# Half of the bf16 quad products and the softmax multiply on GpSimd, and one grouping of the exps throughout

## The chip, the cores and the metric

The kernel runs on one core of a Trainium2 chip. The metric is the device time of one execution in microseconds; the median of several executions is compared. Engines are named as in the profile: PE is TensorE (PEld its weight loads), DVE is VectorE, ACT is ScalarE, POOL is GpSimd, SP is the engine that issues DMAs here.

## The reference

One transformer block with adaptive layer norm: attention with 32 heads of 20 over 2048 tokens of 640, then a bilinear gated unit of width 1536. Everything is bf16.

```python
mod = (_silu(c) @ w_mod).reshape(c.shape[0], 6, 1, -1)
sa, ca, ga, sb, cb, gb = (mod[:, i] for i in range(6))
h = _layernorm(x) * (1 + ca) + sa
qkv = (h @ wqkv).reshape(B, S, 3, 32, 20)           # q, k, v by head
p = _softmax(einsum('bhqd,bhkd->bhqk', q, k) * 20 ** -0.5)
x = x + ga * (einsum('bhqk,bhkd->bhqd', p, v) @ wo)
h = _layernorm(x) * (1 + cb) + sb
x = x + gb * (((h @ w_gate) * (h @ w_up)) @ w_down)
```

(The two middle lines of attention leave out the transposes.) The exponentials are the bulk: 32 heads times 2048 times 2048 scores.

## The kernel before

**Tiling.** The queries are cut into five chunks (`CHUNKS`): three of 512 and two of 256 tokens. The heads are taken four at a time (a set, `j` from 0 to 7), each head in its own 32 rows of the PE array. One chunk and one set make an item; there are 40, taken in order. An item's scores come in units of one PSUM bank: 128 keys by 512 queries, or two times 128 keys by 256 queries. There are 2048 units in all.

**Two ways to an exponential.** Most units go through ACT: exp of a group of two or three neighbouring banks into a buffer `PP` (L1238). The others go through VectorE, four units to a quad (`QUADS` sets how many quads an item has, 93 in all). The queries are scaled beforehand so that a score in PSUM is already in units of a bf16's low bits. For each of the four units, L1262 adds a bias and converts to int16, into one quarter of an input slot of `DB0`. Then three operations over all 2048 elements make two bf16 tensors whose sum, after PV, stands for the exponential: M (L1290) takes the mantissa bits into a slot of `DSS`, X (L1295) multiplies that in place by the same bits read as bf16, and EX (L1298) takes the exponent bits into a second `DSS` slot. `DB0` has two slots (`NB0`), `DSS` three (`NSS`). An input slot is given back when both X and EX have been put in order, and its next user waits for both.

**PSUM.** Exp groups lie alternately in banks 0 to 2 and banks 3 and 4. Bank 7 gathers PV (L1666). Banks 5 and 6 are working banks (`G`), which every projection, transpose and quad unit takes for a while: PE fills one, and VectorE or ACT evicts it. With `HEADG = 60`, the first 60 exp groups have two units each, so that bank 2 isn't needed by them and is a third working bank; it goes back to the exp groups at group 60.

**After PV.** At the end of an item, VectorE transposes bank 7 in 32 by 32 blocks (L1343), takes the reciprocals of the softmax sums (L1346), multiplies (L1348) and transposes back (L1355); DMAs put the result into `Ocp`. When a chunk's items are done, its suffix (output projection, layer norm, gate and up, down projection: L1424 to L1575) is spread over the next chunk's groups; the last chunk's suffix is the tail of the program.

**Projections.** K and V of all tokens and Q of the first chunk are needed early. A K round is either direct (`kq_round`, L878: four heads at 20-row offsets straight into `KT`) or packed (`packed_round`, L929: 128 rows of K at once, stored to DRAM by SP and read back by SP into the layout that the scores need, L978 and L991). `K_DIRECT` names the token tiles (of 512 tokens) whose first set is direct; `K_ALL` those in which all sets are.

**The order.** All of the program is put in order beforehand by a planner in the kernel file (`Sched`). It has a duration for each task, a priority, gates (not before exp group n) and due positions for quad units, and walks through time picking, for each engine, the ready task of the highest priority. The result is one fixed order for each engine with semaphore waits[...]. `steal` (L240) gives ACT an eviction of VectorE's while ACT would be idle, up to `STEAL_END` of the planner's time in ns. Other constants that the change touches: how early K rounds are due (`K_LEAD`, `KD_LEAD`), by which exp group the modulation weights are loaded (`WM_GATE`) and due (`WM_NEED`), how many units a PV batch takes (`PVCAP`), how quads are given precedence (`D_RES`), and how late projections and the suffix are spread (`LATE_L`, `LATEQ_A`, `GATE_F`).

On POOL there are only small things: two memsets of weights, and the layer norms' reciprocal roots on one element per partition (L830, L832, L1445, L1447).

Of the kernel before, what the change touches and what calls it, by code (L numbers as in the profile page):

```python
# [6 lines left out]
ALU = mybir.AluOpType  # L7
AX = mybir.AxisListType
BF16 = mybir.dt.bfloat16
# [12 lines left out]
T0 = 700.0  # L22
DMA_SLOW = 0.0015
DMA_LAT = 1700.0
STEAL_END = 94936.728
STEAL_GAP = 300.0
HAM_W = 3413.3
HAM_MIN = 2550.0
# [85 lines left out]
class Sched:  # L114
# [125 lines left out]
    def steal(self):  # L240
        if self.t > STEAL_END or (self.pend["act"] and self.pend["act"][0][0] < self.t + STEAL_GAP):
            return False
        self.pull("dve")
        best = None
        for task in self.readyl["dve"]:
            if task.alt is not None and (best is None or (task.prio, task.seq) < (best.prio, best.seq)):
                best = task
        if best is None or self.free_at["dve"] <= self.t and best is min(self.readyl["dve"], key=lambda x: (x.prio, x.seq)):
            return False
        if not self.acquire(best, self.t):  # L250
            return False
        self.readyl["dve"].remove(best)
        best.eng = best.ctr = "act"
        best.dur, f = best.alt
        best.emits = [f]
        best.lat = ACT_LAT
        self.finish_issue(best, self.t, best.dur)
        self.free_at["act"] = self.t + best.dur
        self.nsteal += 1
        return True  # L260
# [140 lines left out]
QUADS = [(3, 3, 3, 3, 3, 3, 4, 3), 3, (3, 3, 3, 3, 3, 3, 4, 3), (1, 2, 1, 2, 1, 2, 0, 2), 1]  # L401
D_LEAD = 0.35
NB0, NSS = 2, 3
HEADG = 60
GU_ONE = 0
XCONT = 0
T3_POOL = 0
HEAD_OUT = 1
NPS = 4
TS_4X, TT_2X = 600.0, 1145.0  # L410
WM_GATE = 18
WM_NEED = 1.721
K_DIRECT = (0, 1, 2, 3)
Q_DIRECT = 2
K_LEAD = 0.567
K_ALL = (0, 1)
KD_LEAD = 0.559
DMA_WINDOW = 900000
D_LATE = 12
D_RES = 92  # L420
PVMIN, PVMAX, PVCAP = 2, 11, 18
GATE_F = [0.8, 0.893, 0.938, 0.5, 1.0]
FILL_MIN = 4200.0
DUP_MIN = 0.0
XN_POOL = ()
# [4 lines left out]
HT_L = 0.072  # L430
V_L = 0
LATE_A = 1.174
LATE_L = 2.164
LATEQ = (3,)
LATEQ_A = 7
LATEQ_F = 0.73
QUAD_GAIN = 0.597233983857778
NTERM = 2
# [10 lines left out]
def build_kernel(nc, A_x, A_wqkv, A_wo, B_x, B_w_gate, B_w_up, B_w_down, c, w_mod, out):  # L449
# [14 lines left out]
    sc = Sched()  # L464
# [4 lines left out]
    def at(name, shape, dtype, off):  # L469
        cnt[0] += 1  # L470
        return nc.alloc_sbuf_tensor_at(f"{name}_{cnt[0]}", list(shape), dtype, offset=off, align_bytes=32)
# [79 lines left out]
    DB0 = at("DB0", [128, NB0, 4 * 512], I16, d_off)  # L551
    DSS = at("DSS", [128, NSS, 4 * 512], I16, d_off + NB0 * 4096)
# [65 lines left out]

    G = Slots([5, 6, 2] if HEADG else [5, 6], "G")
    GX = Slots([3, 4] if HEADG else [2, 3, 4], "GX")  # L620
    hx = (1, 3) if HEADG else (1, 3, 4)
    GC = Slots([0, 1], "GC")
# [8 lines left out]
    sB0 = Slots(list(range(NB0)), "B0")  # L631
# [15 lines left out]
    def pool(dur, f, deps=(), prio=3.0, **k):  # L647
        return sc.add(Task("pool", dur, f, deps, prio=prio, **k))
# [27 lines left out]
    def load_wm(v, buf, eng, prio, deps=(), gate=0):  # L676
        d_wm[v] = (dma(eng, 128 * KD * D * 2, lambda e: e.dma_start(buf[:, :, :], wmv[:, :, v * D:(v + 1) * D]),
                       deps, prio=prio, dur=550.0, gate=gate), buf)
# [244 lines left out]
    def k_base(tc):  # L923
        return 80 if tc in K_DIRECT else 0

    def nblk(tc):
        return -(-(D - k_base(tc)) // 128)
# [148 lines left out]
    while ap < NA:  # L1076
        even = len(glist) % 2 == 0
        us = ubuf[ap:ap + (3 if even and len(glist) >= HEADG else 2)]
        apos.append(ap)
# [9 lines left out]
    def need(x):  # L1089
        return 13 + 10 * x  # L1090
    q_zero = {}
    for tc in range(4):
        ln1(tc, 2.0 + tc)
        if tc == 0:
            load_rest()
            load_wm(3, wm_a[0], "sp", 9, [r_sa.last] + chained[-2:-1], WM_GATE)
            load_wm(4, wm_a[1], "sp", 9.1, [r_ca.last] + chained[-1:], WM_GATE + 2)
        hT_rounds(tc, 10 if tc == 0 else need(tc / 4 - HT_L))
# [5 lines left out]
        if tc == 3:  # L1104
            x0_done = [t for l in t_xn.values() for t in l]
    r_sb = col_round(3, 2, need(WM_NEED), False)
    r_cb = col_round(4, 3, need(WM_NEED + .05), True)
    load_wm(2, wm_b[0], "sp", 8, x0_done, WM_GATE + 8)
    load_wm(5, wm_b[1], "sp", 9, x0_done, WM_GATE + 12)

# [19 lines left out]
    sc_use = []  # L1130
    ev_ga = gab_round(2, 0, need(WM_NEED + .5))
    ev_gb = gab_round(5, 1, need(WM_NEED + .55))

    z_oc = [pool(1200, lambda e, i=i: e.memset(Ocp[:, i, KD - 1, :], 0.0), [x for l in tr_last.values() for x in l], prio=9)
            for i in range(2)]
    for tc in range(0 if Q_DIRECT < NSET else 1, 4):
        q_zero[tc] = [dma("sp", 12 * H * 1024, lambda e, tc=tc: e.dma_start(
            bass.AP(QS.tensor, (1024 * tc + DH) * 512, [[32 * 512, H], [512, 12], [1, 512]]),
            Ocp[48:80, 1, KD - 1, :].unsqueeze(1).to_broadcast([H, 12, 512])), [z_oc[1], d_wm[4][0]], prio=9.5,
            dur=720.0, gate=WM_GATE + 20 + 12 * tc)]  # L1140

    for tc in range(4):
        if tc > 0 and tc in K_DIRECT:
            kq_round("K", 0, tc, need(tc / 4))
# [6 lines left out]
    for b in range(4 if Q_DIRECT < NSET else 0):  # L1151
        j0 = -(-(160 + b * 128 - 79) // 80)
        late.append((j0 - .05 - K_LEAD, 2560, lambda p, g, b=b: packed_round("Q", b, 0, p, g)))
    for tc in range(4):
        for j in range(1, NSET if tc in K_ALL else 0):
            late.append((j + tc / 4 - KD_LEAD, 2560, lambda p, g, j=j, tc=tc: kq_round("K", j, tc, p, g)))
        for b in range(0 if tc in K_ALL else nblk(tc)):
            r0 = b * 128 + k_base(tc)
            j0 = max(0 if tc not in K_DIRECT else 1, -(-(r0 - 91) // 80))
            late.append((j0 + tc / 4 - K_LEAD, 2560, lambda p, g, b=b, tc=tc: packed_round("K", b, tc, p, g)))  # L1160
    for t in range(NT):
# [7 lines left out]
    for i, (nd, w, f) in enumerate(late):  # L1169
        even = LATE_A + (NSET - LATE_A) * acc / tot  # L1170
        f(need(nd), int(gi * max(0.0, min(nd - LATE_L, even))))
        acc += w
    ql = [(tc, b) for tc in LATEQ for b in range(KD)]
    for i, (tc, b) in enumerate(ql):
        packed_round("Q", b, tc, 500 + i, int(gstart[1] + LATEQ_A + gpc[1] * LATEQ_F * i / len(ql)), True)

# [3 lines left out]
            prio=10),  # L1180
# [39 lines left out]
    for g, (us, b0) in enumerate(glist):  # L1220
        bset = setA if b0 == 0 else setB
        ems = []
        deps = []
# [32 lines left out]
    for qi, (it, us) in enumerate(dquads):  # L1256
        st_ = d_state[qi]
# [11 lines left out]
    for qi, (it, us) in enumerate(dquads):  # L1269
        st_ = d_state[qi]  # L1270
        st_["src"], st_["ss"] = {}, {}

        def term(f, deps, dur, name, slot=None, src=None, last=False, it=it, qi=qi, st_=st_):
            t = Task("dve", dur, f, deps, prio=2.5 + .001 * qi, name=f"{name}.{qi}")
            if slot is not None:
                t.acq = [(sSS, "s", 1)]
            t.cond = lambda: it <= st_pv["item"]

            def on_t(task):
                if slot is not None:  # L1280
                    st_["ss"][slot] = task.slots["s"]
                if last:
                    sB0.done(st_["slot"], task)
                if src is not None:
                    st_["src"][src] = [task]
            t.on_start = on_t
            return sc.add(t)

        def fm(e, st_=st_):
            return e.tensor_scalar(DSS[:, st_["ss"][0], :], DB0[:, st_["slot"], :], 0x7F, 0x3F00, op0=ALU.bitwise_and,  # L1290
                                   op1=ALU.bitwise_or)

        def fx(e, st_=st_):
            d = DSS[:, st_["ss"][0], :].bitcast(BF16)
            return e.tensor_tensor(d, DB0[:, st_["slot"], :].bitcast(BF16), d, ALU.mult)  # L1295

        def fe(e, st_=st_):
            return e.tensor_scalar(DSS[:, st_["ss"][1], :], DB0[:, st_["slot"], :], 0x7F80, 2, op0=ALU.bitwise_and,  # L1298
                                   op1=ALU.bitwise_or)
        tm = term(fm, list(st_["p1"]), TS_4X, "M", slot=0)  # L1300
        term(fx, [tm], TT_2X, "X", src=0, last=True)
        term(fe, list(st_["p1"]), TS_4X, "EX", slot=1, src=1, last=True)

    first_pv = {}
# [32 lines left out]
    def item_end_tasks(it):  # L1337
# [12 lines left out]
            invT[:, 0:nb32].unsqueeze(2).to_broadcast([128, nb32, 32]), ALU.mult)  # L1350
        if T3_POOL and it < len(items) - 1:
            t3 = pool(n * 2.2 + 200, f3, [t2], prio=0)
# [35 lines left out]
    def suffix(ci):  # L1388
# [17 lines left out]
        def gate(w):  # L1406
            g = gb + 9 + int((gl - 9) * GATE_F[ci] * rc_[1] / w_tot)
            rc_[0] += 1
            rc_[1] += w
            return 0 if tail else g  # L1410
# [324 lines left out]
    def d_wants():  # L1735
        g = pvstate["sidx"]
        return g < NG and dst["next"] < len(dlist) and due[dst["next"]] + D_RES < apos[g]

# [75 lines left out]
    def pick_pe(t):  # L1814
        sc.pull("pe")
        g = pvstate["sidx"]
        if HEADG and g >= HEADG - HEAD_OUT and 2 not in G.gone:
            G.retire(2)
        if g < NG:
            ts, us = score_q[g]  # L1820
            if HEADG and g == HEADG and 2 in G.out:
                ts.deps = ts.deps + G.out.pop(2)
# [154 lines left out]
```

The softmax here doesn't subtract the row's maximum and nothing guards it: scores larger than these inputs give would overflow.

## Time and profile before

| | |
|---|---|
| time, median of 3 (lowest to highest) | 843.85 us (842.52 to 844.39) |
| the profiled execution: time, span | 844.39 us, 842.6 us |
| granted PE clock, mean | 0.986 |
| first exp, end of last exp (timeline) | 17.4 us, 807.8 us |
| exps on ACT; quads; quad units | 683; 93; 372 |
| DMA moved, mean | 52.77 MB, 63 GB/s |

"Busy" is time in which an engine has an instruction under way, and "span" runs from the first instruction to the last. The granted clock is the share of full speed that PE was given. In a row of groups, the figures behind the bar are the group's busy time in us, the mean ns of one instruction, and the idle time of the engine just before them with what ended it.

### The profile page before, as it was taken

To read this page: it belongs to the slowest core of one execution; us is meant where nothing else is said; L and a number is where in the kernel's file an instruction comes from. 1 tells how busy PE (TensorE), PEld (TensorE's weight loads), DVE (VectorE), ACT (ScalarE), POOL (GpSimd) and SP (SyncE) were. 2 spreads that over 40 slices of the span, in tenths; PEclk is the share of its full clock that TensorE was granted. 3 is DMA by queue.
4 is the path that set the end of the run, shared out by engine and by line. 5 is a ranking of instruction groups with operands and counts; after the bars stand their busy time and mean duration, and the time that the engine had idled before them with its cause. 6 is when DMAs were issued, how large, how long until landed. Compare 5 with 4: busy or idle time off the path is not lost.

```text
span 842.6 us, 28098 instructions
## 1 busy us (share of the span) xinstructions
PE 794.3 (94%) x12268; PEld 306.1 (36%) x12268; DVE 714.1 (85%) x1266; ACT 783.0 (93%) x719; POOL 31.6 (4%) x65
## 2 busy tenths in 40 slices
PE   8999989999999999999999999999999999998998
PEld 4433333222233222223333222233244433454477
DVE  7997989888999988898789988989779969677773
ACT  4788999998999999999999999999999999999931
POOL 2300000000002000000002000000000000000000
PEclk9998999998999999999999999999999999999999
DMA  9244210012250122310400211000300237124420
GB/s 300 61 139 118 69 43 17 28 47 84 65 123 15 45 57 64 93 57 22 99 2 5 53 45 44 20 12 13 99 4 5 62 77 135 38 65 95 108 59 19
DMA packets 113890, 52.77 MB, mean 63 GB/s; under 512 B 83232, under 2 KB 113768, under 8 KB 113768
## 3 DMA queue, kind: packets, MB, share of 16 engines
q1 hardware_dynamic: 112839, 49.83, 23.3%
q8 instruction: 97, 1.59, 0.8%
q10 hardware_dynamic: 928, 1.15, 0.4%
q14 instruction: 26, 0.20, 0.1%
HBM read 40.83 MB, written 7.82 MB: 58 GB/s over the span
## 4 chain that ended last, share of the span: by engine, by line
PE 49%; ACT 22%; DVE 20%; issue 8%; POOL 0%; ACTq 0%; DVEq 0%
ACT PP L1238 22%; PE ps_all L768 17%; PE ps_all L1204 15%; PE ps_all L1666 11%; DVE DB L1262 7%; PE ps_all L935 3%; DVE DSS L1295 2%; PE ps_all L883 2%; DVE DSS L1290 1%; DVE st L823 1%; DVE DSS L1298 1%; DVE xck L1432 1%; DVE OT L1343 1%; DVE st L1442 1%; PE ps_all L850 1%
## 5 line engine op out<-in xcount | busy, mean ns | idle before, releaser
L1238 ACT ACTIVATE PP<-ps_all 128x1024 bf16<-128x1024 f32 (+2 forms) x683 | 763.9, 1297 | 11.2 <-PE ps_all L1204 10.3
L1204 PE MATMUL ps_all<-QT,KT 32*128 32x512 bf16 (+1 forms) x2560 | 308.6, 341 | 26.4 <-ACT PP L1238 21.6
L1262 DVE TENSOR_SCALAR DB<-ps_all 128x512 int16<-128x512 f32 x372 | 250.6, 682 | 65.5 <-PE ps_all L1204 63.6
L1204 PEld LDWEIGHTS ps_all<-QT,KT 32*128 32x128 bf16 x2560 | 82.6, 91 | 263.0 <-ACT PP L1238 189.5
L1666 PE MATMUL ps_all<-PP,Vf 128*32 128x512 bf16 (+2 forms) x2112 | 166.4, 345 | 0.6 <-issue 0.4
L768 PE MATMUL ps_all<-h2T,stg 128*32 128x512 bf16 x1440 | 111.2, 382 | 4.8 <-DVE DB L1262 3.4
L1295 DVE TENSOR_TENSOR DSS<-DB,DSS 128x2048 bf16<-128x2048 bf16 x93 | 112.6, 1211 | 0.1
L1666 PEld LDWEIGHTS ps_all<-PP,Vf 128*32 128x32 bf16 (+1 forms) x2112 | 48.0, 94 | 88.5 <-issue 80.2
L1666 PE MATMUL ps_all<-DSS,Vf 128*32 128x512 bf16 (+3 forms) x896 | 75.2, 353 | 0.0
L1290 DVE TENSOR_SCALAR DSS<-DB 128x2048 int16<-128x2048 int16 x93 | 63.3, 681 | 1.4
L1298 DVE TENSOR_SCALAR DSS<-DB 128x2048 int16<-128x2048 int16 x93 | 63.3, 681 | 0.8 <-PE ps_all L1666 0.8
L768 PE MATMUL ps_all<-wd,hprod 128*32 128x320 bf16 x1152 | 57.1, 301 | 1.3 <-DVE DB L1262 0.7
L768 PEld LDWEIGHTS ps_all<-h2T,stg 128*32 128x32 bf16 x1440 | 33.7, 95 | 41.8 <-issue 14.5
L1343 DVE STREAM_TRANSPOSE OT<-ps_all 128x512 f32<-128x512 f32 (+1 forms) x40 | 24.2, 605 | 13.4 <-PE ps_all L1666 13.3
L768 PEld LDWEIGHTS ps_all<-wd,hprod 128*32 128x32 bf16 x1152 | 27.7, 96 | 20.5 <-issue 8.8
L768 PE MATMUL ps_all<-wo,Ocp 128*32 128x320 bf16 x640 | 33.4, 302 | 0.6 <-DVE xck L1432 0.2
L1535 DVE CAST gsb<-ps_all 128x512 bf16<-128x512 f32 (+1 forms) x48 | 29.4, 612 | 4.2 <-PE ps_all L768 4.0
L1445 POOL TENSOR_SCALAR sd<-mv 128x1 f32<-128x1 f32 x14 | 5.8, 416 | 698.9 <-DVE mv L1444 698.9
L768 PE MATMUL ps_all<-wV,hT 128*32 128x320 bf16 x640 | 31.1, 306 | 0.3 <-DVE DB L1262 0.2
L935 PE MATMUL ps_all<-hT,wq 128*32 128x512 bf16 x375 | 30.1, 400 | 1.0 <-DVE DB L1262 1.0
L1666 PEld LDWEIGHTS ps_all<-DSS,Vf 128*32 128x32 bf16 (+1 forms) x896 | 23.1, 96 | 20.8 <-issue 11.0
L1546 DVE TENSOR_TENSOR hprod<-ps_all,gsb 128x512 bf16<-128x512 f32 x36 | 24.6, 682 | 4.4 <-PE ps_all L768 4.1
(108 smaller groups left out, 527.0 us busy)
## 6 DMA issues: line engine op xcount, KB each, us to landing
stg<-in_B_w_gate_dram SPq DMA_DIRECT2D x50, 160.0 KB
stg<-in_B_w_up_dram SPq DMA_DIRECT2D x50, 160.0 KB
QT<-q_rows SPq DMA_DIRECT2D x22, 128.0 KB
wm<-in_w_mod_dram SPq DMA_DIRECT2D x3, 800.0 KB
x<-in_A_x_dram SPq DMA_DIRECT2D x7, 320.0 KB
xck<-in_A_x_dram SPq DMA_DIRECT2D x3, 640.0 KB
wd<-in_B_w_down_dram SPq DMA_DIRECT2D x1, 1920.0 KB
out_dram<-xck SPq DMA_DIRECT2D x12, 160.0 KB
```

The source lines that it names most:

```text
L768: return lambda e, b: e.matmul(ps[32 * x:32 * x + 32, b, c0:c0 + n], lhs()[:, 32 * x:32 * x + 32], rhs(), tile_position=(0, 32 * x), start ...
L935: f = [lambda e, b_, k=k, x=x: e.matmul(ps[x:x + min(32, w - x), b_, :], wx[:, k, r0 + x:r0 + min(x + 32, w)], hT[tc][:, k, :], tile_posit ...
L1204: ems.append(lambda e, i=i, kt=kt: e.matmul(dstf()[:, i * u.n:(i + 1) * u.n], KT[32 * u.s:32 * u.s + 32, u.j, kt * 128:(kt + 1) * 128], QT ...
L1238: return e.activation(PPs[g % 2][:, cellp["p"], 0:nu * 512], ps[:, b0:b0 + nu, :].rearrange("p b c -> p (b c)"), AFT.Exp, scale=ESCALE)
L1262: return e.tensor_scalar(DB0[:, st_["slot"], x * 512:(x + 1) * 512], bank(cell["b"]), EBIAS, 0.0, op0=ALU.add, op1=ALU.max)
L1290: return e.tensor_scalar(DSS[:, st_["ss"][0], :], DB0[:, st_["slot"], :], 0x7F, 0x3F00, op0=ALU.bitwise_and, op1=ALU.bitwise_or)
L1295: return e.tensor_tensor(d, DB0[:, st_["slot"], :].bitcast(BF16), d, ALU.mult)
L1298: return e.tensor_scalar(DSS[:, st_["ss"][1], :], DB0[:, st_["slot"], :], 0x7F80, 2, op0=ALU.bitwise_and, op1=ALU.bitwise_or)
L1343: t1 = Task("dve", n * 1.1 + 70, lambda e: e.transpose(OT[:, 0:n], ps[:, BPV, 0:n]), [], prio=0.0, name=f"T1.{it}")
L1535: f = lambda e: e.tensor_copy(gsb[:, gs, 0:n], ps[:, r.b["b"], 0:n])
L1546: f = lambda e: e.tensor_tensor(hprod[:, fc, 0:n], ps[:, r.b["b"], 0:n], gsb[:, gs, 0:n], ALU.mult)
L1666: ems.append(lambda e, i=i, kt=kt, stt=stt, stp=stp: e.matmul(ps[32 * s:32 * s + mc, BPV, 0:u.n], Vf[:, (kt * H + 4 * u.j + s) * VW:(kt * ...
```

## The change

Four edits. The grouping: `HEADG = 0`, so that exp groups are of three and two banks by turns from the first, banks 5 and 6 are the only working banks while exps run, and bank 2 serves only for some first transposes. The product: for every quad of even number, X is done by POOL in four pieces of 512 elements, each a task of its own with the piece before as its dependency; the input slot is given back with the last piece, and PV of the product waits for it. M and EX of these quads, and all of the others, stay on VectorE. The multiply: with `T3_POOL = 1`, L1348 is done by POOL for every item but the last. The constants: `K_DIRECT` keeps token tiles 0 and 1, so that the first set of tiles 2 and 3 is made by packed rounds as well (their first packed round then starts at row 0 and not at row 80); and others that move due times and gates.

```diff
-STEAL_END = 94936.728
+STEAL_END = 60000.0
...
-HEADG = 60
+HEADG = 0
+X_POOL, X_PIECES, POOL_NS = 2, 4, 2.2
 GU_ONE = 0
 XCONT = 0
-T3_POOL = 0
-HEAD_OUT = 1
+T3_POOL = 1
+HEAD_OUT = 2
...
-WM_GATE = 18
-WM_NEED = 1.721
-K_DIRECT = (0, 1, 2, 3)
+WM_GATE = 16
+WM_NEED = 1.802
+K_DIRECT = (0, 1)
...
-K_LEAD = 0.567
+K_LEAD = 0.577
...
-KD_LEAD = 0.559
+KD_LEAD = 0.431
...
-D_RES = 92
-PVMIN, PVMAX, PVCAP = 2, 11, 18
-GATE_F = [0.8, 0.893, 0.938, 0.5, 1.0]
+D_RES = 100
+PVMIN, PVMAX, PVCAP = 2, 11, 16
+GATE_F = [0.8, 0.95, 0.819, 0.5, 1.0]
...
-LATE_L = 2.164
+LATE_L = 2.08
...
-LATEQ_A = 7
+LATEQ_A = 6
...
         tm = term(fm, list(st_["p1"]), TS_4X, "M", slot=0)
-        term(fx, [tm], TT_2X, "X", src=0, last=True)
+        if X_POOL and qi % X_POOL == 0:
+            deps = [tm]
+            for x in range(X_PIECES):
+                w = 2048 // X_PIECES
+
+                def fxp(e, x=x, w=w, st_=st_):
+                    d = DSS[:, st_["ss"][0], x * w:x * w + w].bitcast(BF16)
+                    return e.tensor_tensor(d, DB0[:, st_["slot"], x * w:x * w + w].bitcast(BF16), d, ALU.mult)
+                t = Task("pool", w * POOL_NS + 150.0, fxp, deps, prio=.1 * qi, name=f"XP.{qi}")
+
+                def on_p(task, x=x, st_=st_):
+                    if x == X_PIECES - 1:
+                        sB0.done(st_["slot"], task)
+                        st_["src"][0] = [task]
+                t.on_start = on_p
+                sc.add(t)
+                deps = [t]
+        else:
+            term(fx, [tm], TT_2X, "X", src=0, last=True)
         term(fe, list(st_["p1"]), TS_4X, "EX", slot=1, src=1, last=True)
```

## The prediction, before the changed kernel was run

> **What bounds the kernel now.** I read the busy times first, then the windows by stage, then the groups, then the waits. The columns of the windows are: stretch, its length, then busy us (instructions) of PE, PEld, DVE, ACT, POOL, then granted clock, DMA share, GB/s.
>
> ```profile
> PE 794.3 (94%) x12268; PEld 306.1 (36%) x12268; DVE 714.1 (85%) x1266; ACT 783.0 (93%) x719; POOL 31.6 (4%) x65
> ...
> 20.00:40.00 20.00, 19.55 (x342) 10.09 (x342) 18.67 (x52) 15.27 (x20) 8.39 (x19) 1.00 0.27 79
> 40.00:60.00 20.00, 19.42 (x269) 7.93 (x267) 18.03 (x29) 16.31 (x21) 0.99 (x2) 0.91 0.42 132
> 60.00:80.00 20.00, 20.00 (x246) 6.26 (x244) 15.51 (x27) 17.08 (x19) 0.00 (x0) 0.83 0.42 110
> 300.00:400.00 100.00, 95.14 (x1267) 30.31 (x1259) 89.42 (x144) 99.98 (x90) 0.00 (x0) 1.00 0.22 60
> 500.00:600.00 100.00, 95.20 (x1240) 30.54 (x1232) 88.30 (x136) 99.98 (x90) 0.00 (x0) 1.00 0.12 30
> 780.00:842.60 62.60, 57.06 (x1624) 39.92 (x1612) 37.70 (x85) 32.30 (x38) 1.22 (x2) 1.00 0.27 63
> ```
>
> Two stages are to be seen. From about 100 to 780 us ACT is full (99.98 of 100): a gain on another engine buys nothing there, and only a delay that reaches ACT counts. Before 100 us PE is full with projections and ACT is idle 3 to 5 us in each 20; exp time lost there is never made good. After the last exp (about 808 us) comes a tail of PE and VectorE work.
>
> ```profile
> L1238 ACT ACTIVATE PP<-ps_all 128x1536 bf16<-128x1536 f32 x311 | 477.0, 1534 | 4.5 <-PE ps_all L1204 3.7 <-PE ps_all L1666 0.2
> L1238 ACT ACTIVATE PP<-ps_all 128x1024 bf16<-128x1024 f32 x371 | 403.0, 1101 | 6.8 <-PE ps_all L1204 6.7
> L1262 DVE TENSOR_SCALAR DB<-ps_all 128x512 int16<-128x512 f32 x372 | 250.6, 682 | 65.5 <-PE ps_all L1204 63.6
> L1295 DVE TENSOR_TENSOR DSS<-DB,DSS 128x2048 bf16<-128x2048 bf16 x93 | 112.6, 1211 | 0.1
> L1290 DVE TENSOR_SCALAR DSS<-DB 128x2048 int16<-128x2048 int16 x93 | 63.3, 681 | 1.4
> L1298 DVE TENSOR_SCALAR DSS<-DB 128x2048 int16<-128x2048 int16 x93 | 63.3, 681 | 0.8 <-PE ps_all L1666 0.8
> L1348 DVE TENSOR_TENSOR OTn<-OT,invT 128x512 bf16<-128x512 f32 x24 | 16.4, 683 | 0.1
> ...
> L883 PE MATMUL ps_all<-hT,wk 128*32 128x512 bf16 x360 | 24.9, 381 | 1.8 <-DVE DB L1262 1.1 <-DVE hT L858 0.6
> ```
>
> ```profile
> DVE DB L1262 <- PE ps_all L1204: 63.6, 80, 2.5
> PE ps_all L1204 <- ACT PP L1238: 21.6, 57, 0.9
> ACT PP L1238 <- PE ps_all L1204: 10.3, 11, 3.0
> PE ps_all L768 <- DVE DB L1262: 6.7, 19, 0.7
> ```
>
> The groups give each operation's price; the waits say that VectorE rarely holds up PE (6.7 us on the largest matmul line), that it waits 63.6 us for scores itself, and that PE waits for ACT more than ACT for PE. The product (L1295) has no consumer in the list of large waits.
>
> [...]
>
> **The change, part by part.** Profiled execution: 844.4 us against a span of 842.6, so 1.8 lie outside; the median is 843.85, 0.5 lower. I work on the profiled one and carry the difference over.
>
> *Exp groups.* 2048 score banks less 372 on VectorE leave 1676. With 60 groups of two and then 2.5 on average: 60 + 1556/2.5 = 683, as counted; without, 671. The pitch near the end is 30.18 us for 27 exps of mean 2.5 banks, 1.118; at 60 us it is 13.36/14 = 0.954 for two banks. The line through these has 0.33 a bank and 0.3 fixed, but the second pitch still holds PE waits; two-bank and three-bank durations (1101, 1534) give 0.433 a bank, so a fixed 1.118 − 1.083 = 0.035 to 0.1. Twelve fewer: −0.4 to −1.2, all where ACT isn't the bound. I take −0.5.
>
> *Two working banks in place of three in the head.* From 33 to 53 us, the line windows count 10 first steps of quads, 4 K or packed rounds, 6 V rounds and 8 transpose rounds. Fill plus eviction by the timeline: 0.39 + 0.68 = 1.07; 1.25 + 0.68 = 1.93; 0.72 + 0.48 = 1.2; 0.4 + 0.6 = 1.0. Together 10.7 + 7.7 + 7.2 + 8.0 = 33.6 bank-us in 20 us, 1.7 banks with no queue; with an estimated 0.5 us for semaphores and half an instruction's queue on each of 28, 47.6, or 2.4 banks. So two banks cost between nothing (16.8 us fits into 20) and 3.8 us here, and perhaps half of that in the neighbouring stretches: 0 to +6, I take +3. DVE at 18 of 20 us makes a queue likely.
>
> *K rounds.* K of token tiles 2 and 3 for the first heads is no longer computed directly: 18 direct rounds (360 matmuls) become 16, while the 10 packed rounds stay. Two rounds of 1.25 us go where PE is full: −2.5. Instead these K tiles go through two DMAs and DRAM; in the timeline the SP queue takes 0.34 for a store and 1.91 for four loads to issue alone. ACT has only 7.9 us of exps between 33 and 53 us, so scores are short just where they come later: 0 to +4, I take +2. The ACT steal limit (95 to 60 us) moves one K eviction of 0.58 us in that range to VectorE: nothing.
>
> *Product on GpSimd, 47 of 93 quads.* VectorE loses 47 × 1.13 (the pitch in the chain) = 53 us, and 24 × 0.6 + 15 × 0.33 = 19 us of L1348, 72 together. [...]
>
> Who waits behind a held instruction: the next L1262 on VectorE, with it a working bank, then PE's next filling of that bank, and the next scores behind it in PE's order. [...] PE is idle 5 us per 100 and the exp buffers cover some. [...] I take one in fifteen, +4 to +5: +4, since 89 of 100 us on VectorE leave room for most.
>
> *Later product.* [...] Quads come every 7.7 us (52 first steps per 100 us) and there are two slots, so it just fits. The order places consumers after a planned 4 × 1.276 = 5.1 us. [...] I take +1. What a lighter VectorE gives back to PE in the calm half of the time: −1. [...]
>
> Sum: −0.5 + 3 − 2.5 + 2 + 4 + 1 − 1 = +6. 844.4 + 6 = 850.4 profiled, about 850 as a median.
>
> **Rivals.**
> 1. [...] Late pieces hold the input slot, the next quad's L1262 blocks at the head of VectorE's order, and PE and ACT follow. [...] Against: only every second quad. At 0.4 us per pool quad through to ACT, 19 us: 862.
> 2. *Faster.* VectorE's relief is real [...]: of the 72 us, enough reaches PE before 100 us, where ACT idles about 12 us, to save 4; the K rounds bring 2.5 and the banks cost 2: 844.4 − 4.5, about 839.5. [...] For it: VectorE 18 to 18.7 of 20 us in the head. Against: few quads lie in the head, and the middle has at most some 4 us of ACT idle to win.
> 3. *Nothing shows.* ACT hides the middle, and banks and K rounds cancel: 844.
>
> **How the numbers follow.** Forecast (845.5 to 856) 0.50, rival 1 (above 856) 0.19, rival 2 (under 842.2) 0.22, rival 3 within 0.2% (842.2 to 845.5, about what a measurement of this kernel can tell from no change) 0.09. Slower is 0.50 + 0.19 = 0.69. The range leaves about 0.08 on either side: 840 to 863. The forecast's own is 845.5 to 856.
>
> **What would show it.** 671 exps; [...] ACT under 99.98 of 100 in the middle; the 33 to 53 us stretch with fewer exps. Wrong would be: ACT still full from 100 us on with the exps ending no later than 808 us; or an exp end put off mostly by a wait for POOL on PE, not by VectorE's queue.

## The result, and the profile after

The changed kernel takes 881.69 us (median of 4, 881.43 to 883.30) against 844.12 (842.52 to 845.03): ratio 1.0451, 95% interval 1.0431 to 1.0472. That is 37.6 us slower, where 6 were forecast. The profiled execution has a span of 879.9 us. One execution each of b_t3, a_h60nopool and a_exfirst below was in a slower state: the ratios leave it out, the medians don't (without it they are 855.05, 846.81 and 885.47 us).

The page of the changed kernel, busy time and chain by engine (chain before: PE 49%, ACT 22%, DVE 20%):

```profile
PE 817.3 (93%) x12272; PEld 313.0 (36%) x12272; DVE 682.7 (78%) x1185; ACT 784.6 (89%) x700; POOL 308.0 (35%) x292
...
PE 49%; DVE 26%; ACT 15%; issue 6%; POOL 1%; DMA 1%; POOLq 0%; ACTq 0%; DVEq 0%
```

VectorE is busy 31 us less, and yet it holds a larger share of the chain; ACT, which was the bound, holds less. Windows of the changed kernel, columns as before:

```profile
20.00:40.00 20.00, 17.21 (x312) 9.00 (x309) 17.32 (x50) 13.12 (x15) 8.27 (x19) 1.00 0.16 43
40.00:60.00 20.00, 17.98 (x233) 6.88 (x225) 13.58 (x22) 11.98 (x11) 4.33 (x5) 0.83 0.35 110
60.00:80.00 20.00, 16.80 (x172) 4.50 (x164) 16.02 (x24) 14.31 (x13) 10.05 (x7) 0.84 0.54 157
...
300.00:400.00 100.00, 96.64 (x1194) 29.43 (x1186) 83.64 (x133) 99.19 (x88) 36.54 (x29) 1.00 0.25 65
...
500.00:600.00 100.00, 94.91 (x1187) 28.71 (x1187) 79.25 (x121) 97.52 (x86) 34.30 (x28) 0.98 0.14 33
```

In the head PE is no longer full (16.8 to 18 of 20 us against 19.4 to 20), and ACT gets less. In the middle VectorE is down to 79 to 84 of 100 us, and ACT is no longer quite full. The groups that answer to those shown before, shapes kept apart:

```profile
L1239 ACT ACTIVATE PP<-ps_all 128x1536 bf16<-128x1536 f32 x335 | 496.8, 1483 | 32.1 <-PE ps_all L1205 21.7 <-PE ps_all L1685 8.8
L1239 ACT ACTIVATE PP<-ps_all 128x1024 bf16<-128x1024 f32 x335 | 355.1, 1060 | 7.1 <-PE ps_all L1205 5.4 <-PE ps_all L1685 1.2
L1263 DVE TENSOR_SCALAR DB<-ps_all 128x512 int16<-128x512 f32 x372 | 251.1, 683 | 96.3 <-PE ps_all L1205 95.5
L1309 POOL TENSOR_TENSOR DSS<-DB,DSS 128x512 bf16<-128x512 bf16 x188 | 235.8, 1254 | 271.7 <-DVE DSS L1291 261.4
L1299 DVE TENSOR_SCALAR DSS<-DB 128x2048 int16<-128x2048 int16 x93 | 79.1, 851 | 0.6 <-PE ps_all L1685 0.6
L1291 DVE TENSOR_SCALAR DSS<-DB 128x2048 int16<-128x2048 int16 x93 | 70.0, 753 | 1.7
L1296 DVE TENSOR_TENSOR DSS<-DB,DSS 128x2048 bf16<-128x2048 bf16 x46 | 56.8, 1235 | 0.0
L1367 POOL TENSOR_TENSOR OTn<-OT,invT 128x512 bf16<-128x512 f32 x24 | 33.8, 1407 | 129.7 <-DVE invT L1365 129.7
```

EX (L1299) has grown from 681 to 851 ns, M (L1291) from 681 to 753. What they lose isn't idle time in front of an instruction (0.6 and 1.7 us in all); it is inside its duration. The view of the one line gives least, median and longest in ns:

```profile
L1299 DVE TENSOR_SCALAR DSS<-DB x93: 630/686/1647, 56.3 to 837.9; 128x2048 int16<-128x2048 int16 x93
```

Before, it was 646/683/694: the median is all but the same, and a few are held. 27 EX, 11 M and 3 X take over 0.06 us more than the longest before, 0.57 us more in the mean; the longest EX takes 0.95 us more, where a GpSimd piece takes 1.155. One of them in the timeline (start and length in us first), with a softmax multiply on GpSimd:

```profile
350.98 1.37 POOL L1367 TENSOR_TENSOR OTn<-OT,invT 128x512 bf16<-128x512 f32 x1 [3.22 <-DVE invT L1365]
...
351.36 1.53 DVE L1299 TENSOR_SCALAR DSS<-DB 128x2048 int16<-128x2048 int16 x1
352.82 0.68 DVE L1263 TENSOR_SCALAR DB<-ps_all 128x512 int16<-128x512 f32 x1
```

The multiply ends at 352.35 us and EX 0.55 later. So it is with all 41: each meets a GpSimd multiply that has more than 0.2 us to go and ends at a set distance behind that multiply's end, 0.55 us for EX and M and 1.08 for X. The 14 EX and M that began with less than 0.2 us of one left took 0.67 to 0.74 us. L1263, which reads PSUM, isn't held: 110 of its 372 began with more than 0.2 us of such a multiply left and took 684 ns in the mean, 693 at most, against 682 for those with no GpSimd work beside them. The texts on record call such a hold a lock.

Counted against undisturbed rows, M, EX and X lose 93 × 0.072 + 93 × 0.170 + 46 × 0.025 = 23.7 us. Other VectorE rows grew as well (the layer norm's xn and xn2t of L1468 by 3.8 us, the scaling of `wo` by 0.7), so that all holds are nearer 28. The waits:

```profile
DVE DB L1263 <- PE ps_all L1205: 95.5, 133, 2.4
...
ACT PP L1239 <- PE ps_all L1205: 27.1, 38, 2.8
...
PE ps_all L1205 <- ACT PP L1239: 11.8, 39, 0.6
...
PE ps_all L769 <- DVE DB L1263: 7.4, 18, 1.0
...
DVE OcT L1374 <- POOL OTn L1367: 4.2, 10, 0.7
```

The relation of ACT and PE is turned round: ACT waits 27.1 us for scores (10.3 before), PE 11.8 for ACT (21.6 before). VectorE waits 95.5 us for scores (63.6 before): it has more time and nothing to do with it. No engine has a wait in the list that the product (L1309) ended.

Where it is lost: exps alone, by stage (columns: stretch, length, ACT busy and instructions, granted clock, DMA share, GB/s). The kernel before, then the changed one:

```profile
0.00:100.00 100.00, 61.03 (x64) 0.93 0.49 140
100.00:240.00 140.00, 136.72 (x122) 0.98 0.19 52
240.00:800.00 560.00, 558.34 (x492) 1.00 0.22 53
```

```profile
0.00:100.00 100.00, 54.61 (x47) 0.91 0.44 130
100.00:240.00 140.00, 126.53 (x111) 0.93 0.19 51
240.00:800.00 560.00, 546.99 (x479) 0.99 0.21 51
```

Exp time missing: 6.4, 10.2 and 11.4 us, 28 in all. The last exp ends at 841.1 us against 807.8, 33.3 later: the other 5 us are that the exps as a whole take 769.1 us and not 763.9. The tail behind the last exp lasts 38.8 us against 34.8, 4.0 more.

### The profile page after: what moved, and what is told of

Its sections match the earlier page's. It is cut to its first block, busy times and chain, and to the rows that moved or that the text cites. A ratio compares the mean times of both kernels' runs of the same rounds, so it can differ in the third digit from the quotient of the medians.

```text
span 879.9 us, 28227 instructions
## 1 busy us (share of the span) xinstructions
PE 817.3 (93%) x12272; PEld 313.0 (36%) x12272; DVE 682.7 (78%) x1185; ACT 784.6 (89%) x700; POOL 308.0 (35%) x292
## 4 chain that ended last, share of the span: by engine, by line
PE 49%; DVE 26%; ACT 15%; issue 6%; POOL 1%; DMA 1%; POOLq 0%; ACTq 0%; DVEq 0%
PE ps_all L1205 16%; PE ps_all L769 16%; ACT PP L1239 15%; PE ps_all L1685 11%; DVE DB L1263 9%; PE ps_all L936 3%; DVE DSS L1291 3%; DVE DSS L1299 2%; PE ps_all L884 2%; DVE OT L1362 1%; DVE DSS L1296 1%; DVE st L824 1%; DVE st L1461 1%; PE ps_all L1923 1%; DMA wm<-in_w_mod_dram 1%
## 5 line engine op out<-in xcount | busy, mean ns | idle before, releaser
L1239 ACT ACTIVATE PP<-ps_all 128x1536 bf16<-128x1536 f32 (+1 forms) x671 | 769.1, 1271 | 39.2 <-PE ps_all L1205 27.1
L1205 PE MATMUL ps_all<-QT,KT 32*128 32x512 bf16 (+1 forms) x2560 | 317.4, 345 | 23.9 <-ACT PP L1239 11.8
L1309 POOL TENSOR_TENSOR DSS<-DB,DSS 128x512 bf16<-128x512 bf16 x188 | 235.8, 1254 | 271.7 <-DVE DSS L1291 261.4
L1263 DVE TENSOR_SCALAR DB<-ps_all 128x512 int16<-128x512 f32 x372 | 251.1, 683 | 96.3 <-PE ps_all L1205 95.5
L1367 POOL TENSOR_TENSOR OTn<-OT,invT 128x512 bf16<-128x512 f32 (+1 forms) x39 | 44.9, 1151 | 205.8 <-DVE invT L1365 205.8
L1299 DVE TENSOR_SCALAR DSS<-DB 128x2048 int16<-128x2048 int16 x93 | 79.1, 851 | 0.6 <-PE ps_all L1685 0.6
L1291 DVE TENSOR_SCALAR DSS<-DB 128x2048 int16<-128x2048 int16 x93 | 70.0, 753 | 1.7
L1296 DVE TENSOR_TENSOR DSS<-DB,DSS 128x2048 bf16<-128x2048 bf16 x46 | 56.8, 1235 | 0.0
L769 PE MATMUL ps_all<-wd,hprod 128*32 128x320 bf16 x1152 | 54.6, 301 | 0.5 <-DVE DB L1263 0.3
L1554 DVE CAST gsb<-ps_all 128x512 bf16<-128x512 f32 (+1 forms) x48 | 29.5, 614 | 11.5 <-PE ps_all L769 11.4
L1923 PE MATMUL ps_all<-ident 128*128 128x512 bf16 x84 | 30.5, 422 | 5.6 <-DVE DB L1263 1.9
L936 PE MATMUL ps_all<-hT,wq 128*32 128x512 bf16 x375 | 32.6, 422 | 2.1 <-DVE DB L1263 0.9
```

The source lines that it names most:

```text
L769: return lambda e, b: e.matmul(ps[32 * x:32 * x + 32, b, c0:c0 + n], lhs()[:, 32 * x:32 * x + 32], rhs(), tile_position=(0, 32 * x), start ...
L936: f = [lambda e, b_, k=k, x=x: e.matmul(ps[x:x + min(32, w - x), b_, :], wx[:, k, r0 + x:r0 + min(x + 32, w)], hT[tc][:, k, :], tile_posit ...
L1205: ems.append(lambda e, i=i, kt=kt: e.matmul(dstf()[:, i * u.n:(i + 1) * u.n], KT[32 * u.s:32 * u.s + 32, u.j, kt * 128:(kt + 1) * 128], QT ...
L1239: return e.activation(PPs[g % 2][:, cellp["p"], 0:nu * 512], ps[:, b0:b0 + nu, :].rearrange("p b c -> p (b c)"), AFT.Exp, scale=ESCALE)
L1263: return e.tensor_scalar(DB0[:, st_["slot"], x * 512:(x + 1) * 512], bank(cell["b"]), EBIAS, 0.0, op0=ALU.add, op1=ALU.max)
L1309: return e.tensor_tensor(d, DB0[:, st_["slot"], x * w:x * w + w].bitcast(BF16), d, ALU.mult)
```

## The experiments

All times are medians, with the kernel before run beside them on the same chip. From chip to chip the median of the kernel before lay between 841.30 and 844.12 us, so that a difference of two runs from different chips is good to some 3 us only. "Held" is what M, EX and X took in the profiled execution beyond 681, 681 and 1210 ns each.

| run | what | us | ratio to before (95%) | held, us |
|---|---|---|---|---|
| after | the change | 881.69 | 1.0451 (1.0431–1.0472) | 23.7 |
| a_nopool | change without GpSimd parts | 853.79 | 1.0127 (1.0099–1.0156) | 0 |
| a_head60 | change with 60 groups of two | 869.87 | 1.0342 (1.0283–1.0401) | 28.2 |
| a_h60nopool | other constants alone | 846.95 | 1.0035 (1.0010–1.0060) | 0 |
| b_head0 | grouping alone, old constants | 861.89 | 1.0233 (1.0199–1.0267) | 0 |
| b_xt3 | both GpSimd parts alone | 871.59 | 1.0352 (1.0320–1.0383) | 23.6 |
| b_x | products alone | 865.50 | 1.0272 (1.0245–1.0299) | 20.4 |
| b_t3 | softmax multiply alone | 856.80 | 1.0148 (1.0103–1.0193) | 9.6 |
| b_dummy | before, idle GpSimd multiplies | 872.53 | 1.0351 (1.0318–1.0383) | 31.7 |
| b_memset | before, idle GpSimd memsets | 847.19 | 1.0059 (1.0040–1.0077) | 4.4 |
| b_pad | before, small VectorE pads | 856.46 | 1.0174 (1.0139–1.0208) | – |
| b_lump | before, few large VectorE pads | 867.93 | 1.0304 (1.0263–1.0345) | – |
| a_cut | after, pieces cut to 8 elements | 869.32 | 1.0331 (1.0302–1.0360) | 3.7 |
| a_cut2 | and the multiply cut | 858.43 | 1.0205 (1.0160–1.0251) | 0 |
| a_memset | after, pieces as memsets | 866.84 | 1.0302 (1.0258–1.0347) | 5.7 |
| a_one | after, one piece | 986.06 | 1.1722 (1.1667–1.1777) | 97.4 |
| a_eight | after, eight pieces | 887.31 | 1.0533 (1.0489–1.0576) | 17.1 |
| a_exfirst | after, EX ahead of M | 885.55 | 1.0479 (1.0407–1.0552) | 19.3 |

**Which part of the change.** Four runs undo a part of the change or do one alone. In their expectations "pool" puts the 37 us down to the GpSimd parts, "banks" to the two working banks.

```diff
a_nopool:  -X_POOL, X_PIECES, POOL_NS = 2, 4, 2.2
           +X_POOL, X_PIECES, POOL_NS = 0, 4, 2.2
           -T3_POOL = 1
           +T3_POOL = 0
```

> The changed kernel with both GpSimd parts undone (products and multiply back on VectorE); grouping and constants stay as changed. Theory 'pool' [...]: 848 to 855 us. Theory 'banks' (they come from two working banks before 240 us): 868 to 880 us. If the two share it about evenly: some 862.

```diff
a_head60:  -HEADG = 0
           +HEADG = 60
           -HEAD_OUT = 2
           +HEAD_OUT = 1
```

> The changed kernel with the first 60 exp groups in two banks each again (three working banks in the head); GpSimd work and constants stay as changed. Theory 'pool': 873 to 880 us. Theory 'banks': 850 to 860 us, with the exps done by 240 us near those of the kernel before (194 against 165).

b_xt3 puts the changed kernel's lines for X into the kernel before, and sets `T3_POOL = 1`.

> The kernel before with the two GpSimd parts alone: products of even quads and the softmax multiply on GpSimd, old grouping and old constants. Theory 'pool': 865 to 880 us, with ACT under 98 of 100 us in the middle. Theory 'banks': 846 to 853 us. [...]

b_head0 sets `HEADG = 0` in the kernel before.

> The kernel before with the grouping alone: groups of three and two from the first, two working banks; no GpSimd work, old constants. Theory 'banks': 862 to 880 us, lost before 240 us. Theory 'pool': 845 to 850 us. The old constants were written down for three banks, so that this kernel may also be slower than the changed one without GpSimd.

In b_xt3 M and EX take 735 and 862 ns. The GpSimd parts cost 881.69 − 853.79 = 27.9 us on top of the new grouping, and 871.59 − 842.60 = 29.0 on top of the old: about the same, whatever the grouping. The grouping and the constants are worth 853.79 − 842.60 = 11.2 us. "Pool" is the larger part and "banks" the smaller; a_head60 (869.87) lies between its two expectations, as both count. A later run took the constants by themselves (`HEADG = 60`, `HEAD_OUT = 1`, `X_POOL` and `T3_POOL` at 0 in the changed kernel):

> The changed kernel with neither the grouping nor the GpSimd parts: what is left of the change are the other constants alone. If they cost nothing: 840 to 846 us, and the grouping is the 11 us between this and 853.8. If they carry a part: 847 to 853 us.

846.95 lies between the two expectations: 4.6 over the 842.32 beside it, 3 by the ratio. So some 7 us are the grouping's with these constants; with the old ones it costs 19.3. The exps of a_nopool by stage show where:

```profile
0.00:100.00 100.00, 52.72 (x46) 0.90 0.44 132
100.00:240.00 140.00, 138.97 (x123) 0.99 0.21 58
240.00:800.00 560.00, 554.52 (x489) 0.98 0.21 52
```

The grouping loses its time before 100 us (52.72 against 61.03, and 62.96 with the constants alone), and nothing between 100 and 240. There PE has 72.9 of the 80 us from 20 to 100 with two working banks, 78.8 with three. The GpSimd parts take theirs after 100 us: 138.97 − 126.53 = 12.4 and 554.52 − 546.99 = 7.5.

**The two GpSimd parts apart.** b_t3 sets `T3_POOL = 1` in the kernel before, b_x brings only the products.

> The kernel before with the softmax multiply alone on GpSimd (39 of 40), products on VectorE. Both theories of the products expect little: 841 to 848 us. [...]

> The kernel before with the products of even quads alone on GpSimd; the softmax multiply stays on VectorE. If the products carry the loss of the GpSimd parts: 865 to 873 us, as both together (871.6).

Both count: 12.5 us (8.7 to 16.3) and 22.9 by the ratios, more than the 29 together. The multiply was a miss. Its 39 operations are on GpSimd for 42 us in all (1.35 and 0.67 us each), yet M and EX are held for 9.6 us, and the transpose back waits 3.6 us for its result (nothing before).

**Hold or late product.** b_dummy keeps the kernel before and its orders and adds GpSimd work for which nobody waits.

```diff
     end = sc.run()
+    prev = None
+    for qi in range(0, len(dquads), 2):
+        tq = d_state[qi]["tm"]          # M of this quad
+        if tq.start < max(x.done for x in ev_ga + ev_gb):
+            continue
+        for w in (448, 448, 448, 448, 256):
+            t = Task("pool", w * 2.2 + 150.0, lambda e, w=w: e.tensor_tensor(
+                scr[:, 0:w], gab[:, 0, 0:w], gab[:, 1, 0:w], ALU.mult), [tq, prev] + ev_ga + ev_gb)
...
```

> The kernel before with its work and its orders on PE, VectorE, ACT and SP kept; 44 even quads (those after the gate vectors are there) have in addition five GpSimd multiplies of 448, 448, 448, 448 and 256 bf16 elements that read a constant tile and write a scratch tile, started by that quad's M. Nothing waits for them but GpSimd itself. Theory 'lock' [...]: 858 to 870 us, and longer rows for M and EX, as in the changed kernel. Theory 'late product' (what costs is the 5 us that the product takes, by which PE's order and the input slot are held): 843 to 848 us.

Groups of b_dummy:

```profile
L1939 POOL TENSOR_TENSOR scr<-gab 128x448 bf16<-128x448 bf16 x176 | 235.6, 1338 | 474.2 <-DVE DSS L1291 463.8
L1296 DVE TENSOR_TENSOR DSS<-DB,DSS 128x2048 bf16<-128x2048 bf16 x93 | 133.1, 1431 | 0.1
L1299 DVE TENSOR_SCALAR DSS<-DB 128x2048 int16<-128x2048 int16 x93 | 73.4, 789 | 0.0
L1291 DVE TENSOR_SCALAR DSS<-DB 128x2048 int16<-128x2048 int16 x93 | 64.3, 692 | 1.4
```

30.4 us slower, with 31.7 us of longer X, EX and M. Here no product is late, no order differs, and no slot is held: the idle multiplies alone do it. Nor is it mainly PE's clock, which was lower in most of these executions: the one with 0.988 took 868.20 us, where the kernel before took 841.36 and 842.05 with 0.988, 26 to 27 us less. The waits of b_dummy show how it gets to ACT (L1668 is PV):

```profile
ACT PP L1239 <- PE ps_all L1205: 27.5, 50, 3.0
...
PE ps_all L1205 <- DVE DB L1263: 9.3, 24, 0.9
...
PE ps_all L1668 <- DVE DSS L1296: 5.5, 11, 1.0
...
PE ps_all L1668 <- DVE DSS L1299: 3.2, 5, 1.0
```

Before, ACT waited 10.3 us for scores and PE's scores 1.5 us for L1262; PV's matmuls had no wait for X or EX. b_memset puts ten memsets in place of the multiplies (`e.memset(scr[:, 0:448], 1.0)`).

> As the run of the kernel before with idle GpSimd multiplies (872.5 us), but with ten GpSimd memsets of 448 elements a quad, which read nothing and write the scratch tile, about 0.5 us each. [...] If a two-input operation is held up only by one that reads SBUF: X stays at 1.21 us, M and EX lengthen, 848 to 858 us. If writing alone holds nothing: 841 to 846 us and no longer rows.

```profile
L1939 POOL MEMSET scr<- 128x448 bf16 x440 | 227.6, 517 | 492.7 <-DVE DSS L1291 470.2
L1296 DVE TENSOR_TENSOR DSS<-DB,DSS 128x2048 bf16<-128x2048 bf16 x93 | 112.5, 1210 | 0.1
L1291 DVE TENSOR_SCALAR DSS<-DB 128x2048 int16<-128x2048 int16 x93 | 64.2, 690 | 1.4
```

With 227.6 us of GpSimd work that reads nothing, X stays at 1210 ns (1225 at most, against 2065 in b_dummy), M is at 690 and EX at 719, and the time is 4.9 us up. So it isn't GpSimd's being busy by itself that hurts. X isn't held at all here. EX still is at times: 15 of them, for 0.21 us in the mean, against 22 for 0.45 us in b_dummy. That fits with the memset being shorter than the multiply (0.517 us against 1.338); whether the missing read spares M and EX anything, this run doesn't tell.

The same in the changed kernel, orders kept: a_cut lets each piece multiply 8 elements (`x * w:x * w + 8`), a_cut2 also cuts the softmax multiply to 32 columns, a_memset makes each piece four memsets of 128.

> The changed kernel with its orders on all engines kept, but each GpSimd piece multiplies 8 of its 512 elements, so that most of these products is left out. Theory 'lock' or late on the chip against the order: back to about 855 to 862 us. Theory 'order' (the loss is in an order that was written down for a 5 us product and would stay whatever GpSimd takes): 874 to 882 us.

> The changed kernel with its orders kept, each GpSimd piece cut to 8 of 512 elements and each softmax multiply on GpSimd cut to its first 32 columns; the rest of both is left out. With almost no time on GpSimd, what is left over 853.8 us (the changed kernel without GpSimd work) is the cost of the order alone. Theory 'lock and late on the chip': 853 to 860 us. Theory 'order': 866 us or more.

> The changed kernel with its orders kept, each GpSimd piece of 512 replaced by four memsets of 128 of its elements[...]; the product is left out. The softmax multiply stays on GpSimd. So the 'product' comes as late as before or later[...]. Theory 'lock': 864 to 872 us, near the run with cut pieces (869.3), and M and EX within 30 ns of 681. Theory 'late product': 878 us or more.

a_cut2 leaves 858.43, 4.6 over a_nopool (6.6 by the ratios): that is left for the order, being written for a product of 5 us. The remaining 881.69 − 858.43 = 23.3 us (20.7 by the ratios) are what GpSimd does on the chip, beside 23.7 us of holds. The near equality of the two sums is in part luck, since the steps don't agree: a_cut takes away 20.0 us of holds and 12.4 us of time, which lies between its two expectations; from there a_cut2 takes away 3.7 us of holds and 10.9 us. With the multiply cut, VectorE's wait for its result also falls (4.5 to 1.1 us), and the granted clock rises (0.968 to 0.976, then 0.978 to 0.988). What each is worth was not tried. a_memset gives back 14.9. Rows of a_memset:

```profile
L1309 POOL MEMSET DSS<- 128x128 bf16 x752 | 145.6, 236 | 288.1 <-DVE DSS L1291 280.5
L1299 DVE TENSOR_SCALAR DSS<-DB 128x2048 int16<-128x2048 int16 x93 | 67.7, 728 | 0.6 <-PE ps_all L1685 0.6
```

A memset took 0.236 us, so the "product" comes earlier than in the change, after 3.8 us at least (16 × 0.236) where that has 5.0, but far later than after the 1.1 of a_cut (4 × 0.276), and the time is that of a_cut or less: lateness of 1.1 to 3.8 us costs nothing that shows. EX missed its 30 ns (728); the softmax multiplies, still on GpSimd, hold EX too (710 in the mean and 1540 at most in a_cut, which keeps them).

**How a wait on VectorE reaches the end.** Without any GpSimd work, VectorE writes a scratch tile ahead of X: b_pad before each of the 93, b_lump before every third.

```diff
     end = sc.run()
+    for t in sc.order["dve"]:
+        if t.name.startswith("X."):                 # b_lump: and int(t.name[2:]) % 3 == 0
+            t.emits = [lambda e: e.memset(scr[:, :], 1.0)] + t.emits
```

> The kernel before, orders kept, no GpSimd work: ahead of each of the 93 products VectorE writes a scratch tile of 320 elements for nothing[...]. Theory 'unplanned VectorE time passes through one for one' (orders are fixed and tight, so mean idle time doesn't help): 866 to 875 us. Theory 'VectorE's idle 11% absorbs it' (then GpSimd harms in some other way than by VectorE's waits): 842 to 850 us.

> The kernel before, orders kept, no GpSimd work: ahead of every third product VectorE writes a scratch tile of 880 one-byte elements for nothing, an estimated 0.9 us, 31 times, 27 to 29 us in all, against 93 times 0.325 us in the run with small pads (856.5 us). Theory 'lumps pass more fully than small pads': 862 to 870 us. Theory 'only the sum counts': 853 to 858 us. If long gaps between pads let the order recover: 845 to 851 us.

The row of the pads in b_pad, then in b_lump:

```profile
L1934 DVE MEMSET scr<- 128x320 bf16 x93 | 30.2, 325 | 1.9
```

```profile
L1934 DVE MEMSET scr<- 128x880 uint8 x31 | 24.6, 792 | 4.2 <-DVE DSS L1291 0.2
```

93 pads of 0.325 us, less the 51 ns by which X gets shorter, are 25.5 us and cost 15.2 (12 to 17 by the interval). 31 of 0.792, less 1.6 us on X, are 23.0 and cost 25.6 (22 to 29). So on this kernel the delays of 0.8 us on VectorE passed through about whole, and those of 0.3 us by half to two thirds, though VectorE has 11 of 100 us free in the middle. Both theories on the record were too extreme for b_pad. The 41 holds of the change, 0.57 us in the mean, lie between the two.

**Length of one hold.** a_one and a_eight set `X_PIECES` to 1 and 8; a_exfirst adds EX ahead of M for the GpSimd quads, with M after it.

> The changed kernel with each GpSimd product in one piece of 2048 elements in place of four[...]. Theory 'lock': the longest M, EX and X on VectorE grow from about 1.6 us to 4 us and more, and the time goes to 895 us or above. Theory 'late product': one piece ends earlier than four (three fixed costs less), so 876 to 882 us.

```profile
L1309 POOL TENSOR_TENSOR DSS<-DB,DSS 128x2048 bf16<-128x2048 bf16 x47 | 198.4, 4221 | 304.2 <-DVE DSS L1291 304.2
L1299 DVE TENSOR_SCALAR DSS<-DB 128x2048 int16<-128x2048 int16 x93 | 153.9, 1655 | 0.4 <-PE ps_all L1685 0.4
L1291 DVE TENSOR_SCALAR DSS<-DB 128x2048 int16<-128x2048 int16 x93 | 70.5, 758 | 1.7
```

104 us slower than the change, with less GpSimd time (198.4 us against 235.8): EX, which comes next after M, waits for most of the piece: the longest takes 4.43 us, 3.75 more than undisturbed. PV waits for EX:

```profile
PE ps_all L1685 <- DVE DSS L1299: 44.5, 20, 3.4
```

In the change that wait is 0.7 us. That a shorter product is so much worse can't be its own lateness.

> The changed kernel with each GpSimd product in eight pieces of 256 elements in place of four of 512; the planner's durations follow. From 0.20 us for 8 elements and 1.155 for 512, a piece takes an estimated 0.67 us. Theory 'lock, by the length of one hold': the longest EX falls from 1.65 to about 1.2 us, its mean from 851 towards 760 ns, and the time to 865 to 876 us. Theory 'late product' or number of GpSimd instructions: 882 us or more.

> The changed kernel with EX ahead of M for the quads whose product is GpSimd's[...]. Theory 'lock': the mean of EX falls from 851 towards 730 ns, and the time by up to 10 us, to 871 to 879. Theory 'late product': the product starts 0.7 us later, so 882 to 890 us.

Holds fell as the lock theory said (17.1 and 19.3 against 23.7; EX's mean with EX first is 769 ns), but the medians did not: 887.31 and 885.55 lie in the ranges written down for "late product". The traces show little of that: PE's matmuls wait 0.7 us for the product in a_eight and not at all in a_exfirst (the weight loads 1.2 and 0.4), and VectorE 6.3 and 8.3 us for the multiply (4.2 in the change). Each has another order on all engines, and a_eight has 277.4 us of products on GpSimd where the change has 235.8. The 19.3 us of a_exfirst are from an execution of 875.56 us with a clock of 0.988, within the lock theory's range; the others took 885.47 to 888.73 with 0.967 to 0.973, and by the intervals this run isn't told from the change. Why eight pieces are not faster stays open. Within one order (after, a_cut, a_memset, a_cut2) the held time predicts the time to some 8 us; from one order to another it doesn't by itself.

## Why the prediction was wrong, point by point

*The bound.* Right in the main: relief on VectorE bought nothing. In a_cut2 VectorE is busy 654.5 us, with nothing held, where a_nopool has 720.0, and the time is no shorter. "From about 100 to 780 us ACT is full" was a little too round: from 200 to 300 us it was busy 96.88 of 100.

*GpSimd's prices.* No wide multiply ran on GpSimd in the kernel before, so the forecast's price of a piece was the author's estimate. Measured, a piece takes 1.155 us in the median and 1.254 in the mean, with waits of its own: 52 of the 188 take over 1.2 us (1.51 in the mean), and each of these met an EX, M, X or xn under way on VectorE and ended 1.01 us after it. POOL is busy 308 us.

*The lock.* That GpSimd's multiplies would hold VectorE was the author's assumption, which no trace of before shows. The runs bear it out: M, EX and X are held (by 72, 170 and 25 ns in the mean), and L1263 isn't (683 ns against 682). What they add is that X is held by GpSimd's multiplies and not by its memsets (1431 ns in b_dummy, 1210 in b_memset). How often and for how long was an estimate too, and too high: on M, EX and X there were 41 holds of 0.57 us, 23.7 us in all, and some 28 with the other rows.

*The step that failed* is how much of it gets through: "I take one in fifteen, +4 to +5: +4, since 89 of 100 us on VectorE leave room for most." Far more got through: 26 to 30 us for 31.7 us of holds in b_dummy, and in the changed order 12.4 for 20.0 with the products alone (a_cut) and 23.3 for 23.7 with both parts. What stood at +4 measured 21 to 23 us. The one in fifteen was of the estimated holds; of the 23.7 us measured it is 1.6. Idle time of VectorE in the mean was taken for slack. It isn't: the orders are fixed, and what is held holds what stands behind it. After 38 of the change's 41 holds the next operation on VectorE began 0.08 us ahead of the held one's end, as it does behind an EX that isn't held. b_dummy shows two ways to ACT. One is the prediction's own: L1263 is late, so a bank comes free late and PE waits with the next scores (9.3 us). The other it did not name: X and EX are late, PV waits for them at the head of PE's order (8.7 us), and the scores stand behind it. How the loss divides between the two was not tried. Idle time that comes later, in a wait for those same scores, doesn't give it back; b_lump shows the loss with no GpSimd at all.

*The later product.* "+1" with the input slot as rival 1's mechanism: the lateness was not shown to cost anything. What is left for the order made for it is some 5 to 7 us. Rival 1 had the right side, but not by the slot: in the list of waits L1263 has none for the product. Its 862 was 20 us too low.

*Head.* Forecast +3 − 2.5 + 2 − 0.5 = +2; measured some 11 with the constants, about 7 of them for the two banks and the grouping alone. The K rounds' −2.5 was too much: the direct rounds went from 360 to 320 matmuls, but the packed ones from 180 to 200. Two banks were mis-sized: the count for one stretch of 20 us (0 to 3.8 us, with 0.5 us for semaphores and queue that was the author's estimate) was taken nearly once, while the profile shows the loss over the whole 20 to 100 us (8.3 us of exp time in a_nopool). What K rounds and their way through DRAM contribute was not tried apart; with the constants they are in the 3 to 4.6 us of a_h60nopool.

*Softmax multiply.* Costed at nothing. In b_t3 it holds M and EX for 9.6 us, and the transpose back waits 3.6 us for its result: some 12.5 us alone.

The sum, re-made: order 4.6, GpSimd on the chip 23.3, grouping and constants 11.2: 39.1, against 37.6 measured. As these are steps from one run to the next, the sum has to close, but for the kernel before (842.60 beside a_nopool, 844.12 here). By the ratios the terms are 6.6, 20.7 and 10.7.

## What to carry to other kernels

In this kernel, work moved from VectorE to GpSimd wasn't free time on VectorE, as 41 of the operations left there were held by GpSimd's multiplies (72 us moved by the prediction's count, and with GpSimd's work on the chip the time some 23 us up): count each meeting, and look for it inside the durations of the held rows. In a program of fixed orders whose engines are 90% busy, don't take an engine's mean idle time for slack: unplanned delays of 0.8 us on VectorE were lost here about in full. Other engines were not tried. A cheap test before such a move is idle work on the new engine, with orders kept and nobody waiting.

## What was not expected of the hardware

X isn't held at all by GpSimd memsets (1210 ns beside 440 of them in b_memset), and M and EX are held by 4.4 us in all. GpSimd's bf16 multiply by length is 0.200, 0.671, 1.155 and 4.063 us in the median for 8, 256, 512 and 2048 elements: some 1.9 ns an element over about 0.19.

PE's granted clock in the profiled execution was 0.986 before, 0.971 in the change and 0.908 in a_one. In the change it was 0.93 between 100 and 240 us (0.98 before), where exps lose most for the length of the stretch. That gaps on PE bring it down is not shown: before, the window from 60 to 80 us has 0.83 with PE busy for all of its 20 us. A part of the loss may go with the clock, in a_one above all (104 us for 73.7 us of additional holds). It isn't the main part: a_head60 took 867.00 us in an execution with 0.996, the kernel before beside it 839.82 with 0.991. How much goes this way was not measured by itself and stays open.
